# One column-tiled key-value burst for both branches, and all W' units moved among the queries of blocks 1 and 2

## The chip, the cores and the metric

One core of a Trainium2 chip. The metric is the device time of one execution in microseconds. Most executions of a kernel agree within 0.3%; all runs below are fast, with a granted TensorE clock of 1.00.

In the profile PE is the TensorE matmul, PEld its weight load, DVE is VectorE, ACT is ScalarE, POOL is GpSimd, SPq is the queue from which SyncE issues DMAs. PSUM is the memory that matmuls write; the program uses it as eight banks of 128 x 512 f32.

## The reference

Two linear-attention branches A and B on the same x, mixed by a gate (sequence 2048, width 640, 32 heads of 20):

```python
qkv = (x @ wqkv)...                         # q, k, v
pq, pk = phi(q), phi(k)                     # phi(t) = (t > 0 ? t + 1 : exp(t)) + 1e-6
kv = einsum("bhsd,bhse->bhde", pk, v);  z = einsum("bhsd->bhd", pk)
num = einsum("bhqd,bhde->bhqe", pq, kv)
den = einsum("bhqd,bhd->bhq", pq, z)[..., None] + 1e-6
branch = (num / den).transpose(...) @ wo
out = g * branch_A + (1 - g) * branch_B,    g = sigmoid((x * gate_w).sum(-1))
```

## The kernel before

The kernel never forms v. It computes G = phi(k)^T x ("g units"), turns it by DMA into GT, multiplies it by the value weights to get all key-value blocks ("key-value steps", `m`), masks them to the head diagonal on VectorE into MB, and multiplies MB by the output weights: W' = kv @ wo, in eleven small units `wp` (five for A, five for B, one for the last two heads of both). The rows of W' then have to change partitions: they go to DRAM (the store `ws`) and come back (the reload `wp` DMA, into WPA or WPB). The queries are computed in four blocks of 512 rows, ten units per block. For two blocks at a time come the denominators (`den`), their reciprocals, a round trip of the factors through DRAM (`fw` writes, `fr` reads into RX), and the scaling of the queries by RX (`ml`). The outputs are the scaled queries times W'.

A query unit is five matmuls into one PSUM bank, an exponential on ScalarE and two VectorE operations, of which the second frees the bank:

```python
mms("q%s%d%d" % (X, b, k), steps, ..., [(tile,)], NC * 518, after=gone[X])
sch.op("ACT", ...activation(ek(), PS[:, tile.banks[0], :], ACT.Exp)...,            name="eq...")
sch.op("DVE", ...tensor_scalar(ek(), ek(), 1.0, EPS, op0=min, op1=add)...,         name="tq...")
sch.op("DVE", ...scalar_tensor_tensor(out=dst, in0=PS[...], scalar=0.0, in1=ek(), op0=max, op1=add)..., name="sq...")
```

A small list scheduler in the kernel orders every operation when the kernel is built, from assumed durations, and also fixes which PSUM banks each one uses. On the chip every engine works off its list in that order:

```python
def _dve_ns(n, rate=1):
    return n / (0.96 * rate) + 68.0
...
def place(x):
    if x.n == 2:      # two adjacent banks, from those not in use in the plan
        c = [(max(r.at[b], r.at[b + 1]), [b, b + 1]) for b in range(0, 8, 2) if not (r.busy[b] or r.busy[b + 1])]
        return min(c) if c else None
...
sch.op("DVE", mask, _dve_ns(n * (q1 - q0)), ...)        # 300 columns: planned at 380 ns
```

The end of the program before the change (cut):

```python
g_unit("B", 0); g_unit("B", 1); m_unit("A"); g_unit("B", 2)
for q in (0, 1): wp_unit("A", q)
...
wp_store("A"); zbd("B")
queries(0)
m_unit("B")
queries(1)                    # the six W' units of B among these; the reload of A is issued here
wp_store("B"); wp_rows("B")
d01 = dens(0)
scale_q(0, d01, 2)
queries(2); queries(3)
scale_q(1, d01, 2)
...
```

## Time and profile before

| | |
|---|---|
| time | 190.78 us median of 3 (190.48 to 190.85) |
| PE busy | 186.3 of 189.7 us |
| two key-value bursts, start to next start | 1.05 and 1.06 us |
| a W' unit on PE | 0.27 to 0.28 us |
| a query unit: PE / ACT / DVE | 1.08 / 0.60 / 0.29 + 0.69 us |
| a wide mask on DVE | 1.03 us; a gate operation behind it starts 0.77 us after it (81.09 to 81.86) |

From the page, its first line and the chain of work that ended last:

```profile
span 189.7 us, 3209 instructions
...
PE 94%; DMA 3%; SPq 1%; DVE 0%; issue 0%; DVEq 0%
```

TensorE is the whole chain once the weights are there. The stages, from the answer on windows (a stretch, its length, then the busy time and number of instructions of PE, PEld, DVE, ACT and POOL, the granted clock, the DMA share, GB/s; cuts at the starts of the first g matmul, of block 0's queries, of the burst of B, of block 1's queries, of the query matmuls after the first denominators, of the first output matmul):

```profile
49.16:95.31 46.15, 46.15 (x387) 39.85 (x386) 20.06 (x54) 8.50 (x16) 0.00 (x0) 1.00 0.17 33
95.31:106.20 10.89, 10.89 (x53) 5.74 (x50) 9.38 (x20) 6.07 (x10) 0.00 (x0) 1.00 0.36 86
106.20:107.26 1.06, 1.06 (x56) 1.03 (x56) 0.97 (x3) 0.60 (x1) 0.00 (x0) 1.00 0.02 8
107.26:123.19 15.93, 15.93 (x96) 9.02 (x93) 13.85 (x29) 10.73 (x18) 0.00 (x0) 1.00 0.36 108
123.19:142.64 19.45, 19.45 (x94) 10.59 (x91) 19.02 (x39) 11.10 (x19) 0.00 (x0) 1.00 0.31 96
142.64:189.70 47.06, 44.96 (x351) 32.04 (x349) 28.68 (x42) 14.67 (x21) 0.00 (x0) 1.00 0.25 79
```

PE is busy for the full length of every stretch but the last.

### The profile page before, as it was taken

The numbers are of one execution on the slowest core, as the hardware profiler recorded it, in microseconds if no ns is written. First come the engines' busy times: TensorE is split into PE (matmuls) and PEld (weight loads), VectorE is DVE, ScalarE is ACT, GpSimd is POOL, SyncE is SP. The second block draws the span as 40 slices with busy tenths as digits, with TensorE's granted clock in tenths as the row PEclk, the third lists the DMA queues.
The fourth block names the chain that finished last, engine by engine and source line by source line (L and its number), as shares of the span: only waits on it lengthen the run. The fifth ranks groups of instructions, "written<-read, shape, count | busy, mean of one in ns | idle before, by whom it ended". The sixth has DMA issues, their size and how long they took to land.

```text
span 189.7 us, 3209 instructions
## 1 busy us (share of the span) xinstructions
PE 186.3 (98%) x1289; PEld 124.0 (65%) x1289; DVE 130.1 (69%) x275; ACT 76.4 (40%) x129; POOL 8.2 (4%) x14
## 2 busy tenths in 40 slices
PE   8999999999999999999999999999999999999995
PEld 3565555555788888888855666455556677777774
DVE  1398989898600009996179997899999959833324
ACT  2255555555311112203255478565553522331332
POOL 8900000000000000000000000000000000000000
DMA  6999699991011111112144004665000173211212
GB/s 184 282 229 202 183 381 371 352 241 43 0 35 38 35 35 38 35 35 38 35 86 111 5 22 173 165 223 171 0 0 3 43 228 92 97 66 46 73 69 69
DMA packets 31936, 21.49 MB, mean 113 GB/s; under 512 B 16818, under 2 KB 31666, under 8 KB 31922
## 3 DMA queue, kind: packets, MB, share of 16 engines
q1 hardware_dynamic: 31490, 20.80, 39.4%
q10 hardware_dynamic: 432, 0.49, 0.8%
q8 instruction: 10, 0.16, 0.4%
q14 instruction: 4, 0.03, 0.1%
HBM read 12.05 MB, written 5.31 MB: 91 GB/s over the span
## 4 chain that ended last, share of the span: by engine, by line
PE 94%; DMA 3%; SPq 1%; DVE 0%; issue 0%; DVEq 0%
PE ps L383 94%; DMA WK<-in_B_wqkv_dram 3%; SPq L372 1%; DVE OL L862 0%; DVEq L276 0%
## 5 line engine op out<-in xcount | busy, mean ns | idle before, releaser
L383 PE MATMUL ps<-WK,XT 128*128 128x512 bf16 (+2 forms) x250 | 44.1, 337 | 0.4 <-DMA WK<-in_B_wqkv_dram 0.2
L383 PE MATMUL ps<-XN,FE 128*128 128x320 bf16 x320 | 44.3, 300 | 0.0
L383 PEld LDWEIGHTS ps<-XN,FE 128*128 128x128 bf16 x320 | 37.5, 117 | 6.0
L383 PEld LDWEIGHTS ps<-WK,XT 128*128 128x128 bf16 x250 | 24.0, 98 | 20.2 <-DMA WK<-in_B_wqkv_dram 1.1
L743 ACT ACTIVATE EK<-ps 128x512 bf16<-128x512 f32 x40 | 23.9, 597 | 18.4 <-PE ps L383 17.4
L563 ACT ACTIVATE EK<-ps 128x512 bf16<-128x512 f32 (+1 forms) x42 | 21.4, 526 | 16.2 <-PE ps L383 16.2
L752 DVE SCALAR_TENSOR_TENSOR FE<-ps,EK 128x512 bf16<-128x512 f32 x40 | 26.8, 688 | 0.7
L856 ACT ACTIVATE TS<-ps,GA 128x640 f32<-128x640 f32 (+2 forms) x18 | 13.1, 735 | 29.3 <-PE ps L383 29.3
L383 PE MATMUL ps<-WPB,FE 128*128 128x320 bf16 (+1 forms) x165 | 24.5, 295 | 0.0
L383 PE MATMUL ps<-WPA,FE 128*128 128x320 bf16 (+1 forms) x165 | 24.5, 295 | 0.0
L573 DVE SCALAR_TENSOR_TENSOR FE<-ps,EK 128x512 bf16<-128x512 f32 (+1 forms) x42 | 23.9, 597 | 0.5
L862 DVE SCALAR_TENSOR_TENSOR OS<-ps,GA,TS 128x640 bf16<-128x640 f32 x15 | 13.0, 870 | 15.2 <-PE ps L383 15.2
L383 PE MATMUL ps<-XT,WQA 128*128 128x512 bf16 x100 | 22.8, 380 | 0.0
L383 PE MATMUL ps<-XT,WQB 128*128 128x512 bf16 x100 | 22.7, 379 | 0.0
L600 ACT ACTIVATE GS<-ps 128x640 bf16<-128x640 f32 x10 | 7.0, 704 | 37.0 <-PE ps L383 37.0
L383 PEld LDWEIGHTS ps<-WPA,FE 128*128 128x128 bf16 x165 | 16.0, 98 | 6.2
L383 PEld LDWEIGHTS ps<-WPB,FE 128*128 128x128 bf16 x165 | 15.8, 98 | 6.2 <-ACT TS L856 0.4
L383 PEld LDWEIGHTS ps<-XT,WQB 128*128 128x128 bf16 x100 | 11.7, 117 | 9.2
L383 PEld LDWEIGHTS ps<-XT,WQA 128*128 128x128 bf16 x100 | 11.6, 118 | 9.4 <-issue 0.4
L705 DVE SCALAR_TENSOR_TENSOR GP<-XN,GWB 128x640 bf16<-128x640 bf16 x16 | 13.3, 828 | 4.1 <-PE ps L383 3.6
L567 DVE TENSOR_SCALAR EK<-EK 128x512 bf16<-128x512 bf16 (+1 forms) x42 | 11.4, 272 | 3.1
L811 DVE TENSOR_TENSOR FE<-FE,RX 128x1280 bf16<-128x1280 bf16 (+1 forms) x20 | 12.6, 686 | 0.9 <-DMA RX<-factor 0.9
(52 smaller groups left out, 80.8 us busy)
## 6 DMA issues: line engine op xcount, KB each, us to landing
out_dram<-OS SPq DMA_DIRECT2D x15, 160.0 KB, 1.8
XN<-in_A_x_dram SPq DMA_DIRECT2D x3, 640.0 KB, 8.4
factor<-RC SPq DMA_DIRECT2D x4, 256.0 KB, 2.6
RX<-factor SPq DMA_DIRECT2D x4, 256.0 KB, 3.0
WVA<-in_A_wqkv_dram SPq DMA_DIRECT2D x1, 800.0 KB, 10.8
WQA<-in_A_wqkv_dram SPq DMA_DIRECT2D x1, 800.0 KB, 12.2
WVB<-in_B_wqkv_dram SPq DMA_DIRECT2D x1, 800.0 KB, 11.2
WQB<-in_B_wqkv_dram SPq DMA_DIRECT2D x1, 800.0 KB, 12.2
```

Source lines behind the costliest of these rows:

```text
L372: ins = e.dma_start(dst() if callable(dst) else dst, src() if callable(src) else src, transpose=transpose)
L383: ins = pe.matmul(o, l, r, start=a, stop=z, tile_position=tp, skip_group_check=True)
L563: "ACT", lambda e, ps=ps, ek=ek: e.activation(ek(), ps(), ACT.Exp), _act_ns(n), reads=[(tile,)], writes=[(es,)],
L567: "DVE", lambda e, ek=ek: e.tensor_scalar(ek(), ek(), 1.0, EPS, op0=ALU.min, op1=ALU.add), _dve_ns(n, 4),
L573: return e.scalar_tensor_tensor(out=out, in0=two(ps()), scalar=0.0, in1=two(ek()), op0=ALU.max, op1=ALU.add)
L600: "ACT", lambda e: e.activation(GS[:, k, :].rearrange("p (h f) -> p h f", f=HALF), pair(tile, HALF), ACT.Copy),
L705: lambda e, t=t: e.scalar_tensor_tensor(out=GP[:, :], in0=XN[:, t, 0:D], scalar=1.0, in1=GWB[:, :], op0=ALU.mult, op1=ALU.mult, accum_out= ...
L743: "ACT", lambda e: e.activation(ek(), PS[:, tile.banks[0], :], ACT.Exp), _act_ns(512), reads=[(tile,)],
L752: lambda e: e.scalar_tensor_tensor(out=dst, in0=PS[:, tile.banks[0], :], scalar=0.0, in1=ek(), op0=ALU.max, op1=ALU.add),
L811: return e.tensor_tensor(out=v, in0=v, in1=RX[:, xs.slot, 512 * x + w * j : 512 * x + w * j + w].unsqueeze(1).to_broadcast([128, NC, w]), ...
L856: "ACT", lambda e: e.activation(t_ap(), acc(), ACT.Copy, scale=GA[:, 0, t : t + 1]), _act_ns(hi - lo),
L862: lambda e: e.scalar_tensor_tensor(out=o_ap(), in0=acc(), scalar=GA[:, 1, t : t + 1], in1=t_ap(), op0=ALU.mult, op1=ALU.add),
```

## The change

The intent: two key-value bursts become one, behind the queries of block 0, with the odd last group of A and of B side by side in different column groups of the array; all eleven W' units go among the queries of blocks 1 and 2 and are copied by ScalarE; the scaling of block 0 is written behind the queries of block 2. The core of the diff:

```diff
-WPLAG = 2
+WPAT = (2, 4, 5, 7, 8, 10, 12, 13, 15, 16, 18)
-        MB = sb("MB", [128, 6, 120])
+        MB = sb("MB", [128, 11, 120])
-        def m_unit(X):
+        def m_both(after):
...
+                r = [step(x, q, g, j) for x in (0, 1) for q in range(5) for j in range(NC) for g in (0, 1)]
+                return r + [step(x, 5, x, j) for j in range(NC) for x in (0, 1)]
...
+            for x, q0, q1, g, w in ((0, 0, 5, 0, 12), (0, 0, 5, 1, 12), (0, 5, 6, 0, 8), (1, 5, 6, 1, 8), (1, 0, 5, 0, 12), (1, 0, 5, 1, 12)):
...                                        # the six masks, one after the other
-        g_unit("B", 0)
-        g_unit("B", 1)
-        m_unit("A")
-        g_unit("B", 2)
-        for q in (0, 1):
-            wp_unit("A", q)
...
+        for k in range(NC):
+            g_unit("B", k)
+        order = [0, 1, 2, 3, 4, 10, 5, 6, 7, 8, 9]
...
+                    i = 10 * (b - 1) + 5 * (X == "B") + k
+                    if i in WPAT:
+                        i = WPAT.index(i)
+                        wp_unit(order[i])
+                        if i == 5:
+                            wp_store("A")
                             wp_rows("A")
+                        if i == 10:
+                            wp_store("B")
+                            wp_rows("B")
...
-        queries(0)
-        m_unit("B")
+        m_both(queries(0))
         queries(1)
-        wp_store("B")
-        wp_rows("B")
-        d01 = dens(0)
+        d01, _ = dens(0)
+        queries(2)
         scale_q(0, d01, 2)
-        queries(2)
         queries(3)
```

More of the change, by code (lines that the diff above doesn't have):

```diff
@@ L406, in bass_gated_mix__linear_attn_block__linear_attn_block__prompt_kernel @@
         sch.op("POOL", lambda e: e.memset(W5[:, :], 0.0), 500, writes=[("W5", X) for X in XS], name="w5z")
-        sch.op("POOL", lambda e: e.memset(MB[:, :, :], 0.0), 700, writes=[("M", q) for q in range(6)], name="mz")
+        sch.op("POOL", lambda e: e.memset(MB[:, :, :], 0.0), 700, writes=[("M", q) for q in range(11)], name="mz")
         def load_x(eng, t):
@@ L620, in zbd, with step, mask @@
             )
-        def m_unit(X):
-            tile = _Tile(1)
-            last = XS.index(X)
-            def steps():
-                r = []
-                for q in range(6):
-                    w = 12 if q < 5 else 8
-                    for j in range(NC):
-                        for g in (0, 1) if q < 5 else (last,):
-                            at = D * j + 120 * q + 60 * g * (q < 5)
-                            r.append((
-                                PS[64 * g : 64 * g + 64, tile.banks[0], 60 * q : 60 * q + NC * w], WV[X][:, at : at + 64],
-                                GT[X][:, j, :, 24 * q + 12 * g * (q < 5) : 24 * q + 12 * g * (q < 5) + w], j == 0, j == NC - 1, (0, 64 * g),
-                            ))
-                return r
-            mms("m%s" % X, steps, [("GT", X, k) for k in range(NC)] + [("WV", X), ("WVP", X)], [(tile,)], 25 * 75 + 400)
-            for q0, q1, g, w in ((0, 5, 0, 12), (0, 5, 1, 12), (5, 6, last, 8)):
+        def m_both(after):
+            tiles = [_Tile(1), _Tile(1)]
+            def step(x, q, g, j):
+                w, lo = (12, 12 * g) if q < 5 else (8, 0)
+                at = D * j + 120 * q + DH * lo // 4
+                return (
+                    PS[64 * g : 64 * g + 64, tiles[x].banks[0], 60 * q : 60 * q + NC * w], WV[XS[x]][:, at : at + 64],
+                    GT[XS[x]][:, j, :, 24 * q + lo : 24 * q + lo + w], j == 0, j == NC - 1, (0, 64 * g),
+                )
+            def steps():
+                r = [step(x, q, g, j) for x in (0, 1) for q in range(5) for j in range(NC) for g in (0, 1)]
+                return r + [step(x, 5, x, j) for j in range(NC) for x in (0, 1)]
+            mms(
+                "m", steps, [("GT", X, k) for X in XS for k in range(NC)] + [("WV", X) for X in XS] + [("WVP", X) for X in XS],
+                [(t,) for t in tiles], 110 * 38 + 240, after=after,
+            )
+            for x, q0, q1, g, w in ((0, 0, 5, 0, 12), (0, 0, 5, 1, 12), (0, 5, 6, 0, 8), (1, 5, 6, 1, 8), (1, 0, 5, 0, 12), (1, 0, 5, 1, 12)):
                 n = DH * (w // 4)
-                def mask(e, q0=q0, q1=q1, g=g, w=w, n=n):
+                o0 = 10 if q0 == 5 else 5 * x
+                def mask(e, x=x, q0=q0, q1=q1, o0=o0, g=g, w=w, n=n):
                     p0 = 64 * g
@@ L647, in mask @@
                     return e.tensor_tensor(
-                        out=MB[p0 : p0 + n, q0:q1, 60 * g : 60 * g + n].rearrange("p q (i k) -> p q k i", k=NC),
-                        in0=PS[p0 : p0 + n, tile.banks[0], 60 * q0 : 60 * q0 + n * (q1 - q0)].rearrange("p (q k i) -> p q k i", k=NC, i=w),
+                        out=MB[p0 : p0 + n, o0 : o0 + q1 - q0, 60 * g : 60 * g + n].rearrange("p q (i k) -> p q k i", k=NC),
+                        in0=PS[p0 : p0 + n, tiles[x].banks[0], 60 * q0 : 60 * q0 + n * (q1 - q0)].rearrange(
+                            "p (q k i) -> p q k i", k=NC, i=w
+                        ),
                         in1=m.unsqueeze(1).to_broadcast([n, q1 - q0, NC, w]), op=ALU.mult,
@@ L653, in m_unit, with ws, wp_unit @@
                 sch.op(
-                    "DVE", mask, _dve_ns(n * (q1 - q0)), reads=[(tile,), ("CB",)], writes=[("M", q) for q in range(q0, q1)],
-                    name="mm%s" % X,
-                )
-        def wp_unit(X, q):
+                    "DVE", mask, _dve_ns(n * (q1 - q0)), reads=[(tiles[x],), ("CB",)], writes=[("M", q) for q in range(o0, o0 + q1 - q0)],
+                    name="mm%d" % x,
+                )
+        def ws(u):
+            return GS[0:120, u, :] if u < 5 else WS[:, u - 5, :]
+        def wp_unit(u):
             tile = _Tile(2)
-            w = W5 if q == 5 else WO[X][:, q, :]
+            X = XS[min(u // 5, 1)]
+            w = W5 if u == 10 else WO[X][:, u % 5, :]
             def steps():
                 return [
-                    (PS[0:120, tile.banks[h], 0:HALF], MB[0:124, q, :], w[0:124, HALF * h : HALF * h + HALF], True, True, None)
+                    (PS[0:120, tile.banks[h], 0:HALF], MB[0:124, u, :], w[0:124, HALF * h : HALF * h + HALF], True, True, None)
                     for h in (0, 1)
@@ L669, in wp_unit @@
             mms(
-                "wp%s%d" % (X, q), steps, [("M", q)] + [("W5", Y) for Y in XS if q == 5] + [("WO", X, g) for g in (0, 1) if q < 5],
+                "wp%d" % u, steps, [("M", u)] + [("W5", Y) for Y in XS if u == 10] + [("WO", X, g) for g in (0, 1) if u < 10],
                 [(tile,)], D + 60,
             )
-            dst = WS[:, q, :].rearrange("p (h f) -> p h f", f=HALF)
-            def src():
-                return PS[0:120, tile.banks[0] : tile.banks[1] + 1, 0:HALF]
-            name = "wpe%s%d" % (X, q)
-            if X == "A" and q % 2 == 0:
-                sch.op("DVE", lambda e: e.tensor_copy(dst, src()), _dve_ns(D), reads=[(tile,)], writes=[("WS", q)], name=name)
-            else:
-                sch.op("ACT", lambda e: e.activation(dst, src(), ACT.Copy), _act_ns(D), reads=[(tile,)], writes=[("WS", q)], name=name)
+            sch.op(
+                "ACT",
+                lambda e: e.activation(
+                    ws(u).rearrange("p (h f) -> p h f", f=HALF), PS[0:120, tile.banks[0] : tile.banks[1] + 1, 0:HALF], ACT.Copy
+                ),
+                _act_ns(D), reads=[(tile,)], writes=[("WS", u)] + [("GS", u)] * (u < 5), name="wpe%d" % u,
+            )
         def wp_store(X):
+            u0 = 5 * XS.index(X)
             dma(
-                "SP", "ws" + X, WD[X].ap()[0:600, :].rearrange("(q p) f -> p q f", p=120), WS[:, 0:5, :], reads=[("WS", q) for q in range(5)],
-                writes=[("WD", X, 0)], us=2.0,
+                "SP", "ws" + X, WD[X].ap()[0:600, :].rearrange("(q p) f -> p q f", p=120), (GS[0:120, :, :] if X == "A" else WS[:, 0:5, :]),
+                reads=[("WS", u) for u in range(u0, u0 + 5)], writes=[("WD", X, 0)], us=2.0,
             )
@@ L693, in wp_rows @@
             p0 = 60 * XS.index(X)
-            dma("SP", "ws5" + X, nat[600:D, :], WS[p0 : p0 + 40, 5, :], reads=[("WS", 5)], writes=[("WD", X, 5)], us=0.2)
+            dma("SP", "ws5" + X, nat[600:D, :], WS[p0 : p0 + 40, 5, :], reads=[("WS", 10)], writes=[("WD", X, 5)], us=0.2)
             dma(
@@ L739, in steps @@
                 ]
-            mms("q%s%d%d" % (X, b, k), steps, [("XTC", t, c) for t in range(4 * b, 2) for c in range(NC)] + [("XT", t) for t in range(max(2, 4 * b), 4 * b + 4)] + [("WQ", X)], [(tile,)], NC * 518, after=gone[X])
+            o = mms("q%s%d%d" % (X, b, k), steps, [("XTC", t, c) for t in range(4 * b, 2) for c in range(NC)] + [("XT", t) for t in range(max(2, 4 * b), 4 * b + 4)] + [("WQ", X)], [(tile,)], NC * 518, after=gone[X])
             sch.op(
@@ L756, in q_unit @@
             )
+            return o
         def dens(b0):
@@ L773, in den @@
                 return r
-            mms(
+            o = mms(
                 "den%d" % b0, den, [("ZBD", X) for X in XS] + [("PQ", X, k, b) for X in XS for k in range(NC) for b in (b0, b0 + 1)],
@@ L778, in dens @@
             )
-            return dtile
+            return dtile, o
         def scale_q(b, dtile, pieces):
@@ L905, in bass_gated_mix__linear_attn_block__linear_attn_block__prompt_kernel @@
         gates()
-        g_unit("B", 0)
-        g_unit("B", 1)
-        m_unit("A")
-        g_unit("B", 2)
-        for q in (0, 1):
-            wp_unit("A", q)
-        g_unit("B", 3)
-        for q in (2, 3):
-            wp_unit("A", q)
-        g_unit("B", 4)
-        wp_unit("A", 4)
-        wp_store("A")
+        for k in range(NC):
+            g_unit("B", k)
         zbd("B")
+        order = [0, 1, 2, 3, 4, 10, 5, 6, 7, 8, 9]
         def queries(b):
@@ L921, in queries @@
                 for k in range(NC):
-                    q_unit(X, b, k)
-                    q = 5 * (X == "B") + k - WPLAG
-                    if b == 1 and 0 <= q < 6:
-                        wp_unit("B", (q - 1) % 6)
-                        if q == 0:
+                    o = q_unit(X, b, k)
+                    i = 10 * (b - 1) + 5 * (X == "B") + k
[4 more added lines that the diff above has]
+                            wp_store("A")
                             wp_rows("A")
+                        if i == 10:
+                            wp_store("B")
+                            wp_rows("B")
+            return o
         def finals(b):
@@ L934, in finals @@
                     final(t, ((0, 320), (320, 480), (480, D)), {320: 0, D: 320})
-        queries(0)
-        m_unit("B")
+        m_both(queries(0))
         queries(1)
-        wp_store("B")
-        wp_rows("B")
-        d01 = dens(0)
+        d01, _ = dens(0)
+        queries(2)
         scale_q(0, d01, 2)
-        queries(2)
         queries(3)
         scale_q(1, d01, 2)
-        d23 = dens(2)
+        d23, _ = dens(2)
         finals(0)
```

## The prediction

> **What bounds it.** TensorE, with no slack. The page has PE busy 186.3 of 189.7 us; the chain of waits is one PE piece from 9.39 to 187.26 us. By starts in the timeline, 25 query matmuls of 512 columns start 95.31 to 100.71, 216 ns each, which agrees with the Trainium skill ("TensorE: Matmul & The Clock Gate", Back-to-back issue gap: N/2.4 + 2.5 ns, so 215.8). The 320-column ones take 137 ns. Only PE work removed, or a new PE wait, can move the time.
>
> **What the change does to PE.** Nothing is removed: 110 key-value matmuls and 22 W' matmuls stay. Before, the two key-value bursts stand at 79.78 to 80.83 and 106.20 to 107.26. From the end of streaming of the neighbour before (79.69, 106.11) each costs about 1.14 us: about 0.1 us to get in (and, estimated, 0.1 out), the rest 55 matmuls. From the count in flight in narrow windows I estimate 16 ns per matmul in alternating column groups and 26 ns in the five of the odd group, which run alone. The skill ("TensorEngine Tiling (Array Packing)", Key Properties) says that a change of tiling mode drains the array; the 0.09 us gaps agree. One burst of 110 with the odd groups of both branches alternating: 110 x 16 ns + 0.2 = 2.0 us, against 2.28. Gain 0.3 us. W' units cost 0.27 to 0.28 us both among the g units and among the queries: moving them gains nothing.
>
> **ScalarE.** Three DVE copies (0.82 us) become ScalarE copies (0.70 us). The query exponential is 0.60 per 1.08 us query; with a copy every second query ScalarE stays under 90%. Before shows this (111 to 118 us) without a PE wait.
>
> **VectorE.** It gets six masks at once after the burst. A 60x300 mask is 1.03 us (0.78 start to start) where the scheduler plans 0.38. Masks take about 3.5 us, planned 1.74. Query work is 0.93 us back to back, against 1.08 to 1.35 us of PE per query, so the lag of the query results should be gone by the seventh (estimate). Until then seven of eight PSUM banks are held at most, and the first W' has its mask a microsecond early. The denominator matmuls come after that and keep their small slack. I expect no PE wait, but this is the risk.
>
> **W' of B arrives later.** Last unit at about 130.5, copied by 131.5; the store took 5.0 us and the reload 4.2, so it lands at about 141. The first output matmul with it is at 143.7. That is 2.5 us of margin, against 16 before.
>
> **Sum.** 190.78 - 0.3 = 190.5 us; within 2% almost surely. Range 189.9 to 191.3: the upper side holds a PE wait of up to 1 us. Faster by over 2%: 0.01; within 2%: 0.96; slower by over 2%: 0.03.
>
> **What would show it.** One burst of 110 at about 103.6 us lasting 1.9 to 2.0 us between its neighbours; g units of B without gaps, ending near 92.8; queries at 216 ns; six masks in a row on VectorE at about 105.8; first output matmul 0.2 to 0.4 us earlier than 142.64; no PE wait on DVE or on the reload of W'.
>
> **What would make it wrong.** A PE wait on masks, on banks or on the denominators' operands (0.3 to 1.5 us); the reload landing after the first outputs are due (1 to 3 us); drains costing more than I read, so that one switch fewer saves more.

## More of the kernel before

SyncE's queue around the first factors (start, length of the issue, what):

```profile
123.72 0.35 SPq L372 DMA_DIRECT2D WPB<-wrowsB  x1
125.59 2.31 SPq L372 DMA_DIRECT2D factor<-RC  x2
128.70 1.70 SPq L372 DMA_DIRECT2D RX<-factor  x2
```

The read of a factor waits in this queue until its write has landed, so 125.59 to 128.70, 3.1 us, is the write.

In the VectorE timeline the four scalings of block 0 follow:

```profile
131.47 3.03 DVE L811 TENSOR_TENSOR FE<-FE,RX 128x1280 bf16<-128x1280 bf16 x4 [0.37 <-DMA RX<-factor]
```

They wait 0.37 us for RX.

## The result, and the profile after

| | before | after |
|---|---|---|
| time, median | 190.64 us (190.48 to 190.85, 4 runs) | 193.29 us (193.07 to 193.41, 4 runs) |
| ratio | | 1.0137 (95%: 1.0119 to 1.0155) |
| profiled span | 189.7 us | 192.0 us |
| first g matmul to the end | 140.54 us | 143.46 us |

A ratio here is the mean time of one kernel's fast runs over the mean of the other's of the same rounds, so not quite the ratio of the medians. The change is 1.4% slower: within 2%, as was also forecast, but outside the predicted 189.9 to 191.3. The last row is the better measure of a stage: how soon the first weights arrive moves the first g matmul by up to 1 us from one profiled run to the next (48.4 to 49.4 us over the runs), whatever was changed. I call it *the rest of the run* below.

The page after, and the windows with the same cuts:

```profile
span 192.0 us, 3202 instructions
...
PE 78%; DVE 11%; DMA 7%; SPq 1%; issue 0%; ACT 0%; DVEq 0%
```

```profile
48.54:92.14 43.60, 43.60 (x322) 37.58 (x321) 16.76 (x49) 7.30 (x13) 0.00 (x0) 1.00 0.17 35
92.14:103.03 10.89, 10.89 (x53) 5.74 (x50) 8.66 (x19) 6.08 (x10) 0.00 (x0) 1.00 0.08 15
103.03:104.88 1.85, 1.85 (x111) 1.82 (x110) 1.69 (x4) 0.60 (x1) 0.00 (x0) 1.00 0.00 0
104.88:121.90 17.02, 16.14 (x99) 8.94 (x93) 15.23 (x30) 10.84 (x18) 0.00 (x0) 1.00 0.15 37
121.90:144.08 22.18, 21.00 (x104) 11.86 (x101) 19.44 (x38) 14.67 (x25) 0.00 (x0) 1.00 0.55 168
144.08:192.00 47.92, 45.17 (x350) 31.96 (x350) 28.48 (x42) 14.06 (x20) 0.00 (x0) 1.00 0.24 78
```

The g stage lost one burst and five W' units, as meant. The fourth stretch holds the same PE work in both kernels (twelve query units, six W' units, the denominators): it grew by 1.09 us. The fifth has five W' units more, 1.38 us, but grew by 2.73: 1.35 too many. The last holds the same work and grew by 0.86. In the PE timeline (the bracket is the idle time before the group and what ended it) the three places are:

```profile
108.43 2.32 PE L383 MATMUL ps<-XT,WQA 128*128 128x512 bf16 x10
111.63 0.48 PE L383 MATMUL ps<-WOA,MB 124*120 124x320 bf16 x2 [0.88 <-DVE FE L758]
...
137.34 5.56 PE L383 MATMUL ps<-XT,WQB 128*128 128x512 bf16 x25
144.08 1.52 PE L383 MATMUL ps<-WPA,FE 128*128 128x320 bf16 x10 [1.19 <-DVE FE L758]
146.22 1.52 PE L383 MATMUL ps<-WPB,FE 128*128 128x320 bf16 x10 [0.61 <-DVE FE L758]
```

Counted by starts (ten matmuls of 0.216 us from 108.43 end at 110.59, and so on), they cost 1.04, 1.34 and 0.78 us: waits W1, W2 and W3, together 3.16. The burst gives back 0.35: from the end of the last query's streaming (97.54 + 25 x 0.216 = 102.94) to 104.88 it takes 1.94 us, against 1.14 and 1.15 for the two before. 3.16 - 0.35 = 2.81, of the 2.92 measured; most of the remaining 0.1 us is the slower start after waits (the W' unit behind W1 takes 0.32 us instead of 0.28, the output group behind W3 1.50 instead of 1.45).

All three waits end with L758, the VectorE operation `sq` that frees a query's bank. So it is VectorE that came late, twice. The first time (VectorE timeline):

```profile
104.99 3.77 DVE L649 TENSOR_TENSOR MB<-ps,CB 60x300 bf16<-60x300 f32 x5
108.51 0.37 DVE L753 TENSOR_SCALAR EK<-EK 128x512 bf16<-128x512 bf16 x1
108.91 1.03 DVE L649 TENSOR_TENSOR MB<-ps,CB 60x300 bf16<-60x300 f32 x1
109.96 0.69 DVE L758 SCALAR_TENSOR_TENSOR FE<-ps,EK 128x512 bf16<-128x512 f32 x1
110.57 0.28 DVE L753 TENSOR_SCALAR EK<-EK 128x512 bf16<-128x512 bf16 x1
110.88 0.69 DVE L758 SCALAR_TENSOR_TENSOR FE<-ps,EK 128x512 bf16<-128x512 f32 x1
```

The five masks in a row and the sixth hold it until 109.94. From the chain of waits, which lists them singly (start, length):

```profile
104.99 1.03 DVE MB L649
...
106.05 1.05 DVE MB L649
...
107.11 0.27 DVE MB L649
```

A mask behind a mask starts only when the first has ended, 1.06 us after it. The scheduler orders two reads of one PSUM tile and makes each mask wait for the one before; the operation behind the fifth, a `tq`, has no such wait and overlaps it (107.73 to 108.51). That the wait is the reason is not shown, though. The `sq` behind the sixth mask does not wait for it in the program either, and yet starts only at its end (109.94 to 109.96). Run e10 has the same kind of operation behind a wide mask twice, both times without a wait on it:

```profile
109.33 1.02 DVE L649 TENSOR_TENSOR MB<-ps,CB 60x300 bf16<-60x300 f32 x1
110.11 0.76 DVE L758 SCALAR_TENSOR_TENSOR FE<-ps,EK 128x512 bf16<-128x512 f32 x1
110.90 1.03 DVE L649 TENSOR_TENSOR MB<-ps,CB 60x300 bf16<-60x300 f32 x1
111.97 0.69 DVE L758 SCALAR_TENSOR_TENSOR FE<-ps,EK 128x512 bf16<-128x512 f32 x1
```

The first mask works on the partitions from 0 on, and the next operation starts 0.78 us after it; the second works on those from 64 on, and the next operation starts 1.07 us after it. In the row of masks the two kinds alternate, so that this, and not the wait, can be what spaces them; no run was made to separate the two. For TensorE it comes to this: the second `sq` of block 1 ends at 111.57; W1 ends at 111.63. The second time:

```profile
130.06 0.29 DVE L753 TENSOR_SCALAR EK<-EK 128x512 bf16<-128x512 bf16 x1
132.96 0.82 DVE L818 TENSOR_TENSOR FE<-FE,RX 128x1280 bf16<-128x1280 bf16 x1 [2.61 <-DMA RX<-factor]
133.71 0.69 DVE L758 SCALAR_TENSOR_TENSOR FE<-ps,EK 128x512 bf16<-128x512 f32 x1
```

VectorE stands 2.61 us before the first scaling (0.37 before the change), though the `tq` of the next query ended at 130.35 and its `sq` could have run. The Trainium skill ("TensorE: Matmul & The Clock Gate", the table at its head) has the queue of VectorE as strict first-in first-out; the trace agrees, the ready `sq` starts only at 133.71, behind the scaling. And the reason for the late RX is in SyncE's queue:

```profile
123.88 0.36 SPq L372 DMA_DIRECT2D WPA<-wrowsA  x1
124.30 2.31 SPq L372 DMA_DIRECT2D factor<-RC  x2
130.12 1.12 SPq L372 DMA_DIRECT2D RX<-factor  x2
```

The reload of W' of A, 800 KB, is now issued 0.4 us ahead of the first factor write, which takes 5.8 us (before: 3.1, with the reload of B 1.9 us ahead of it).

The slack can be read from the plan that the kernel's own scheduler makes at build time (planned start, unit, banks, and the VectorE operation it waits for):

```
after    109.38 wp1  banks 2,3  waits sq of A, unit 1, block 1  (planned end 108.31)
after    140.40 fA0  banks 2,3  waits sq of B, unit 0, block 3  (planned end 139.35)
after    141.76 fB0  banks 0,1  waits sq of B, unit 2, block 3  (planned end 141.49)
before   140.45 fA0  banks 4,5  waits sq of A, unit 3, block 3  (planned end 138.16)
before   141.81 fB0  banks 6,7  waits sq of B, unit 1, block 3  (planned end 140.37)
```

fA0 and fB0 are the first output matmuls. Their planned slack was 2.29 and 1.44 us and is 1.05 and 0.27.

The theory: (1) six masks planned at 1.74 us and lasting 5 make the second W' unit wait for its pair of banks, W1; (2) the reload of A delays the factor write, VectorE stands before the first scaling, and the plan's thin slack at the outputs passes that on to TensorE, W2 and W3. Rivals: VectorE is late at the outputs because of the masks; or because of where the scalings now stand in its order, not because of the DMA.

### The profile page after: what moved, and what is told of

Read it like the earlier page. It is cut to its first block, busy times and chain, and to the rows that moved or that the text cites. A ratio compares the mean times of both kernels' runs of the same rounds, so it can differ in the third digit from the quotient of the medians.

```text
span 192.0 us, 3202 instructions
## 1 busy us (share of the span) xinstructions
PE 186.0 (97%) x1289; PEld 123.8 (64%) x1289; DVE 128.6 (67%) x272; ACT 78.3 (41%) x132; POOL 8.7 (5%) x14
## 4 chain that ended last, share of the span: by engine, by line
PE 78%; DVE 11%; DMA 7%; SPq 1%; issue 0%; ACT 0%; DVEq 0%
PE ps L383 78%; DVE FE L758 4%; DMA factor<-RC 3%; DMA WK<-in_B_wqkv_dram 3%; DVE MB L649 2%; DVE FE L818 2%; DMA RX<-factor 1%; SPq L372 1%; DVE EK L753 1%; DVE RC L800 1%; DVE OL L869 0%; ACT DN L794 0%; DVEq L276 0%
## 5 line engine op out<-in xcount | busy, mean ns | idle before, releaser
L383 PE MATMUL ps<-XN,FE 128*128 128x320 bf16 x320 | 43.8, 300 | 0.0
L758 DVE SCALAR_TENSOR_TENSOR FE<-ps,EK 128x512 bf16<-128x512 f32 x40 | 27.1, 688 | 0.8
L383 PE MATMUL ps<-XT,WQB 128*128 128x512 bf16 x100 | 23.2, 379 | 0.0
```

Source lines behind the costliest of these rows:

```text
L383: ins = pe.matmul(o, l, r, start=a, stop=z, tile_position=tp, skip_group_check=True)
L758: lambda e: e.scalar_tensor_tensor(out=dst, in0=PS[:, tile.banks[0], :], scalar=0.0, in1=ek(), op0=ALU.max, op1=ALU.add),
```

## The experiments

Most of them leave the plan alone and move single operations afterwards, between scheduling and emission (`shift` takes operations out of an engine's list and puts them behind a named one), so that TensorE has the same order and the same banks. "Rest" is first g matmul to the end, from the profile.

| run | time, us | before, same rounds | ratio | rest, us | PE waits W1, W2, W3 as the profile lists them |
|---|---|---|---|---|---|
| before | | | | 140.54 | none after the start |
| after | 193.29 | 190.64 | 1.0137 | 143.46 | 0.88, 1.19, 0.61 |
| e1_late_reload | 191.47 | 190.71 | 1.0035 | 141.29 | 0.87, -, - |
| e2_cheap_masks | 192.14 | 190.71 | 1.0079 | 142.29 | -, 1.13, 0.61 |
| e3_scale_later | 192.17 | 190.71 | 1.0071 | 141.99 | 0.88, -, 0.50 |
| e9_scale1_later | 191.96 | 190.71 | 1.0059 | 141.82 | 0.88, 0.17, - |
| e5_masks_between | 192.90 | 190.84 | 1.0100 | 142.87 | 0.54 (elsewhere), 0.94, 0.61 |
| e6_both | 191.08 | 190.84 | 1.0008 | 140.94 | 0.53 (elsewhere), -, - |
| e4_before_reload_at_factor | 192.09 | 190.84 | 1.0065 | 141.96 | 0.65 and 0.17 (elsewhere) |
| e8_other_queue | 194.76 | 190.84 | 1.0201 | 143.81 | 0.87, 1.54, 0.61 |
| e10_honest | 190.13 | 190.61 | 0.9984 | 140.21 | none |
| e7_old_order | 192.96 | 190.61 | 1.0127 | 142.87 | 0.88, -, 1.25 |

### e1: the reload of A behind the factor reads

```diff
         sch.schedule()
+        shift("SP", ("wpA",), "fr1")
```

> The changed kernel with one thing moved: the reload of W' of A is issued behind the reads of the factors of blocks 0 and 1, not ahead of their writes; TensorE, VectorE and ScalarE run the very same instructions in the same order and banks. Theory (the reload holds up the factor write, VectorE stands 2.6 us at the first scaling, its query results come late and the first output matmuls wait for banks): write of the factor to its read falls from 5.8 to about 3 us, VectorE's wait for RX from 2.6 to under 0.5, the two PE waits before the first outputs (1.3 and 0.8 us) vanish, the first PE wait (about 1 us at 111) stays: 193.3 - 2.1 = 191.2 us. Rival A (VectorE is late because of the six masks or because the scalings of block 1 stand ahead of query results in its order): RX arrives earlier, time stays within 0.4 us of 193.3.

Measured 191.47 us; the rest of the run shrank by 2.17 us (143.46 - 141.29), as much as W2 and W3 together. SyncE's queue, and VectorE at the first scaling (no wait is listed before it):

```profile
124.56 2.31 SPq L372 DMA_DIRECT2D factor<-RC  x2
127.23 2.17 SPq L372 DMA_DIRECT2D RX<-factor  x2
129.51 0.43 SPq L372 DMA_DIRECT2D WPA<-wrowsA  x1
```

```profile
130.53 0.82 DVE L818 TENSOR_TENSOR FE<-FE,RX 128x1280 bf16<-128x1280 bf16 x1
```

The write takes 2.7 us and VectorE no longer waits. TensorE's and VectorE's lists and banks are those of the change, so the place of the reload is what W2 and W3 need to appear; the rival that puts them down to VectorE's order or to the masks alone falls.

### e2: cheap masks (wrong result)

```diff
-  out=MB[p0 : p0 + n, o0 : o0 + q1 - q0, ...], in0=PS[..., 60 * q0 : 60 * q0 + n * (q1 - q0)], in1=m...[n, q1 - q0, NC, w]
+  out=MB[p0 : p0 + n, o0 : o0 + 1, ...],       in0=PS[..., 60 * q0 : 60 * q0 + n],             in1=m...[n, 1, NC, w]
```

> The changed kernel, wrong on purpose: each of the four wide masks copies one of its five 60-column pieces, with the plan left as it was, so only the true durations of the masks shrink (1.03 to an estimated 0.3 to 0.4 us). Theory: the PE wait of about 1.1 us at 111 vanishes, the two waits before the first outputs stay at about 2.1 us together: 192.2 us. Rival A (the six masks make VectorE late all the way to the outputs): the later waits shrink too, 190.5 to 191.3 us. Rival B (the first wait is not of the masks): 193.3 us.

Measured 192.14 us (relative error 0.85, as meant; only the masks' true length changed). W1 is gone, W2 and W3 stand at 1.13 and 0.61 us. The rest shrank by 1.17. So W1 is the masks', and W2 and W3 are not.

### e3: the scalings of block 0 later in VectorE's order

```diff
+        shift("DVE", ("mlA0", "mlB0"), "sqB24")
```

> The changed kernel with the four scalings of block 0 moved behind the last query result of block 2 in VectorE's order; reload and factor write as in the change. Theory: the factors still come at about 132.9 us, but VectorE has query results to do meanwhile and no longer stands idle 2.6 us; the waits before the first outputs fall from 2.1 to about 0.6 us together: about 191.8 us. Rival A (VectorE has too much work in that stretch, wherever it stands): 193.3 us.

The factor write is still slow (5.6 us, 124.57 to 130.13), but VectorE has query results to do meanwhile. W2 is gone and W3 is 0.50 us, the 0.6 that was expected together; the rest shrank by 1.47. The time, 192.17, is 0.4 above the expected one: the rest of the run, 141.99, is the expected 143.5 - 1.5, so the difference lies in the start. The same amount of VectorE work in the same stretch costs 1.5 us less when the late operation does not stand first in the line.

### e9: the scalings of block 1 behind the last query results

```diff
+        m = [o for o in sch.order["DVE"] if o.name in ("mlA1", "mlB1")]
+        m[0].name = m[1].name = "early1"
+        shift("DVE", ("early1",), "sqB34")
```

> The changed kernel with the two scalings of block 1 that stand ahead of the query results of block 3 moved behind the last of them, as the kernel before has them; reload untouched. Theory with thin slack: VectorE's wait of 2.6 us for RX stays, but 0.75 and 1.5 us less stand ahead of the results whose banks the first two output matmuls take; the waits fall from 2.1 to 0.6 us together, 191.8 us. If the late factors alone set it and the order does not matter: 193.3 us.

Measured 191.96 us. VectorE's wait for RX is still there (2.9 us at most), yet W2 is 0.17 and W3 gone; the rest shrank by 1.64. So the order of VectorE sets how much of the delay reaches TensorE: of the 2.17 us that the late factors cost (e1), about 0.5 are left here. (The kernel before is a little different: one scaling of block 1 still stands ahead of its last query result, 144.22 before 144.96.) How much the order of the kernel before absorbs is seen in e4.

### e4: the kernel before, with its reload held until the factor write

```diff
         sch.schedule()
+        w = next(o for o in sch.ops if o.name == "wpB")
+        w.deps[next(o for o in sch.ops if o.name == "rc0")] = True
...
```

> The kernel before, with only the reload of W' of B held until the first reciprocal is done, so that it is issued just ahead of the factor writes (before: 1.9 us ahead of them). Theory: the write of the factor to its read grows from 3.1 to 5 to 6 us, VectorE stands 2 to 3 us at the first scaling (before 0.4), and, as the kernel before has more slack in its banks (an estimated 1.2 to 2.3 us), the PE waits before the first outputs sum up to about 1 to 1.4 us: 191.7 to 192.1 us against 190.7. If the late reload is harmless in itself: 190.7.

The cause, put into the other kernel. SyncE's queue:

```profile
125.23 0.35 SPq L372 DMA_DIRECT2D WPB<-wrowsB  x1
125.62 1.87 SPq L372 DMA_DIRECT2D factor<-RC  x2
130.72 1.13 SPq L372 DMA_DIRECT2D RX<-factor  x2
```

```profile
133.55 3.03 DVE L811 TENSOR_TENSOR FE<-FE,RX 128x1280 bf16<-128x1280 bf16 x4 [2.86 <-DMA RX<-factor]
```

The write went from 3.1 to 5.1 us, VectorE waits up to 2.9 us for RX, and the time is 192.09 against 190.84, as expected. The PE waits came in part earlier than I thought: counted by starts, 0.81 us at a query unit of block 3 that needs a bank, and 0.54 before the second output group and the second denominators. The rest grew by 1.42 us. So with its wider planned slack the kernel before absorbs only a part: VectorE's wait grows by 2.5 us and TensorE loses 1.42, where the change loses 2.17 to a wait of 2.6. The thin slack of the change makes the loss larger, but the loss does not need it.

### e8: the reload from another queue

```diff
+        w = next(o for o in sch.ops if o.name == "wpA")
+        sch.order["SP"].remove(w)
+        sch.order["POOL"].append(w)
+        w.eng = "POOL"
```

> The changed kernel with the reload of W' of A issued by the GpSimd engine's queue at about the same moment, the factor writes by SyncE as before. If the factor write is late because it stands behind the reload in one queue: write to read falls to about 3 us and the time to 191.2 to 191.5 us. If the two share the DMA engines whatever the queue: write to read stays at 4.5 to 6 us and the time at 192.5 to 193.3 us.

SyncE's queue:

```profile
125.14 2.31 SPq L372 DMA_DIRECT2D factor<-RC  x2
131.46 1.12 SPq L372 DMA_DIRECT2D RX<-factor  x2
```

The reload is issued by GpSimd at 125.11 us, and the factor write, alone in SyncE's queue, takes 6.3 us; the time is 194.76, above both expected ranges. So it is not the order within SyncE's queue. The Trainium skill ("Trainium Kernel Development and Optimization", Key Constraints) says that DMAs issued from the SP, ACT and POOL queues all run on the same 16 DMA engines and interleave; this run agrees, but it does not single the engines out: the two transfers meet in DRAM as well. What helps is a different time (e1); this different queue does not, and ScalarE's was not tried. (Its time is 1.5 us above that of the change, its rest of the run only 0.35, which is W2's growth to 1.54 us. In the profiled run the first g matmul came 0.85 us later, and about 0.5 us lie outside the profiled span: in all four runs of e8 the time exceeds the span by 1.84 to 1.88 us, in those of the other kernels by 1.26 to 1.39. I looked into neither.)

### e7: the scaling of block 0 written where it was

```diff
+        scale_q(0, d01, 2)
         queries(2)
-        scale_q(0, d01, 2)
```

> The changed kernel with the scaling of block 0 put back ahead of the queries of block 2 in the program, as before (the last part of the change undone); this gives a somewhat different plan. Rival (the moved scaling is the cause of the later waits): they vanish, 191.2 us. Theory (the reload ahead of the factor write): VectorE still stands 2 to 3 us at the first scaling and the PE waits before the outputs sum up to 1 to 2 us, 192.3 to 193.3 us.

Measured 192.96 us: VectorE still stands 2.7 us at the first scaling, and PE waits 1.25 us at the second output group. The moved line of the program is not the cause.

### e5 and e6: the masks of B among the query results, without and with the late reload

```diff
+        b = [o for o in sch.order["DVE"] if o.name == "mm1"]
+        b[0].name, b[1].name, b[2].name = "mb5", "mb0", "mb1"
+        shift("DVE", ("mb5", "mb0"), "sqA10")
+        shift("DVE", ("mb1",), "sqA11")
```

> The changed kernel, right results, with the three masks of branch B moved behind the first and second query result of block 1 in VectorE's order; engines otherwise as they were, the reload where the change has it. Theory: the second query result is out early enough that the second W' unit finds its pair of banks free, the PE wait of 0.9 us at 111 goes or falls under 0.3 us, the two before the first outputs stay (1.2 and 0.6 us): 192.2 to 192.4 us. Rival (the wait is of anything else than the order of masks and query results): 193.3 us.

> The masks of B between the query results and the reload of W' of A behind the factor reads, together. Theory: no PE wait over 0.3 us is left after the key stage, and only the gain of the single burst stands: 0.3 us under the kernel before, 190.4 against 190.7 us, ratio 0.998. If moving the W' units or the burst costs something that I have not named, the ratio is 1.001 or more.

A partial miss. The second W' unit no longer waits, but the next query unit does: its bank is the one that the key-value results of B are in, and it now waits 0.54 us for the last mask, 0.69 us counted by starts. (The profile of e5, e6, e4 and e8 also lists 0.18 us of idle time right behind the burst. That is a record missing from the trace: the group there has 14 matmuls instead of 15, and from the start of the burst to the first W' unit it is 5.12 us in e5 as in the change.) e5 is at 192.90 us, and e6 at 191.08, level with the kernel before (ratio 1.0008, interval 0.999 to 1.0026). Its rest of the run adds up: 140.54 - 0.35 + 0.69 = 140.88, measured 140.94. Moving the masks in a fixed plan moves the wait; the banks have to be planned with them.

### e10: true mask lengths in the scheduler, and the late reload

```diff
-                    "DVE", mask, _dve_ns(n * (q1 - q0)), ...  name="mm%d" % x,
+                    "DVE", mask, 800 if q0 == 0 else 300, ... name="mm%d" % x, lat=400.0,
...
+        shift("SP", ("wpA",), "fr1")
```

> The changed kernel with the scheduler told 800 ns for a wide mask and 300 ns for a narrow one, with 400 ns to its result (it had 380 and 110, with 180), and the reload of W' of A behind the factor reads. The plan keeps TensorE's order of work but gives the second W' unit the banks of the first, and spreads the masks among query results. Theory: no PE wait over 0.2 us between the burst and the outputs; from the first key-sum matmul to the end 140.2 us (before 140.54, the change 143.46), the gain of the one burst; the time 0.3 to 0.4 us under the kernel before, ratio 0.998. If one mask or bank is still late: 0.3 to 0.7 us more.

The list of PE's waits has one line left, at the start of the program:

```profile
PE ps L383 <- PEq L985: 0.8, 1, 0.8
```

The rest of the run is 140.21 us, 0.33 less than before, and the time 190.13 against 190.61 us, ratio 0.9984 (0.9967 to 1.0000). With the true lengths the scheduler gives the second W' unit the banks of the first, which ScalarE frees, and spreads the masks. The order on TensorE is not quite kept: the third W' unit comes one query unit later than in the change. This is the fastest kernel, by the 0.3 us that were forecast for the burst; the interval just reaches 1, so the gain in time is likely rather than certain, while the stage measure shows it plainly.

## Why the prediction was wrong

It said 190.5 us, 189.9 to 191.3; it was 193.3.

- *"One burst of 110 ... 110 x 16 ns + 0.2 = 2.0 us, against 2.28. Gain 0.3 us."* Right: 1.94 us against 2.29, and e10 shows the gain in the end.
- *"W' units cost 0.27 to 0.28 us ... moving them gains nothing."* Right on PE; the ScalarE copies cost no PE wait either.
- *"Masks take about 3.5 us, planned 1.74."* The size was off: 104.99 to 109.94, 5.0 us. The 0.78 us start to start was read from a mask with another kind of operation behind it; a mask behind a mask starts 1.06 us after it, and the sixth came behind a query operation as well.
- **The step that failed first:** *"Until then seven of eight PSUM banks are held at most, and the first W' has its mask a microsecond early ... I expect no PE wait."* I counted free banks and looked at the first W' unit. The plan fixes which banks each unit takes, and the second W' unit had the pair that the first two queries of block 1 free, behind the masks: it waited 1.04 us by starts (W1). e2 took the masks' length away and W1 went. In e10, where the unit has other banks, W1 is gone too, but there the masks are spread as well.
- **The step that failed most:** *"no PE wait on DVE or on the reload of W'"*, for which the prediction looked at the DMAs only in *"W' of B arrives later ... 2.5 us of margin"*: it asked only when their data is there. That part held: the reload of B was issued at 137.25 us, took 4.1 and delayed nothing. What it did not ask is what the moved transfers collide with. The reload of A moved from 113.61 to 123.88 us, 0.4 us ahead of the first factor write, which then took 5.8 us instead of 3.1. That set VectorE back by 2.6 us at an operation that it cannot pass, and the outputs waited 2.1 us (W2 and W3). e1 and e4 show that the place of the reload does this in both kernels, e8 that it is not the order within SyncE's queue. That the shared DMA engines are the reason fits, but is not shown.
- *"no PE wait on DVE"* also relied on the slack before. The new plan had 1.05 and 0.27 us at the first outputs where the old one had 2.29 and 1.44; e9 shows that with two scalings placed later most of the delay is absorbed. The late factors are what W2 and W3 need: with the same thin slack and early factors there is no wait (e1, e10). The thin slack is not needed for a loss: in e4 the kernel before loses 1.42 us to late factors with its old slack.

What stays open: why 5.8 us and not less. The transfers share the engines, but no run here separates the packets of the write that stand behind those of the reload. And why the masks stand 1.06 us apart: the wait that the program has, or the partitions.

## What to carry to other kernels

When a change moves a large transfer, ask not only whether its data comes in time but which smaller transfer that something waits for it now stands beside; the round trip of factors through DRAM (256 KB each way) was such a one, and another queue for the reload did not help here. On an engine that works in order, a late operand costs everything behind it, so give operations that wait on a DMA a place where something ready stands ahead of them. Where a scheduler fixes order and banks at build time, check its assumed durations against the trace before moving work: a mask planned at 0.38 us that takes 1.05 turned a correct gain of 0.3 us into a wait of 1.

## What the Trainium skill lacked or had wrong

- "TensorE: Matmul & The Clock Gate" (Wait — 56ns, not 53.3ns?) says that start-to-start never drops below about 25 ns. That holds here only within a column group: the 110 matmuls of 60 and 40 columns of the burst, which alternate between two groups, start within 1.74 us (103.03 to 104.77), 32 ns apart in each group and 16 ns apart on average over both.
- "TensorE: Matmul & The Clock Gate" (Back-to-back issue gap), which the prediction cites, gives N/2.4 + 2.5 ns for an isolated matmul and about 131 ns for one of 512 columns in a stream of weight loads and matmuls. The query matmuls are such a stream, and take 216 ns each (25 of them, 95.31 to 100.71): the formula fits and the 131 ns do not.
- "TensorEngine Tiling (Array Packing)" (Key Properties) says that a change of tiling mode drains the array but gives no size. Here the gap between the last query's streaming and the first column-tiled matmul is about 0.09 us (102.94 to 103.03).
- "Trainium Kernel Development and Optimization" (Key Constraints) states the sharing of the 16 DMA engines, but no page read gives its price for a smaller transfer. A factor write took 2.7 us with nothing large beside it, 3.1 with an 800 KB reload issued 1.9 us ahead, 5.1 to 5.8 with one 0.4 to 0.5 us ahead, and 6.3 with one from another queue at the same moment.
- "VectorE: DVE Perf Modes" (The DRAIN you can't avoid) says that the next operation does not start until the pipe is empty, and that one that is not held starts earlier. Its next section (Two Vector instructions with no wait between them) models which operation is held by the quarter of the partitions at which inputs and outputs start. The spacings here fit that model, though no run was made to test it: without a wait in the program an operation starts 0.78 us after a wide mask on the partitions from 0 on (109.33 to 110.11 in e10) and 1.07 us after one on those from 64 on (110.90 to 111.97). Neither number stands on the page, and a plan of VectorE needs both.
